# Two loads swapped, a stretch of the FFN in another array form, and the steps in a new order: retention followed by a gated FFN

## The chip, the cores and the metric

The kernel runs on one core of one Trainium2 chip. The metric is device microseconds of one execution, the median of three runs.

## The reference

Two operations follow each other. The first is a retention layer, written as a recurrence over 768 tokens for 4 sequences and 8 heads of 64 columns:

```python
for t in range(S):
    state = gamma * state + einsum('bhd,bhe->bhde', k[:, :, t], v[:, :, t])
    y[:, :, t] = scale * einsum('bhd,bhde->bhe', q[:, :, t], state)
```

The second is a feed-forward network on the 3072 resulting rows of 512 columns, with 1536 hidden columns: `out = (sigmoid(x @ w_gate) * (x @ w_val)) @ w_out`.

## The kernel before

**Tiling.** A tile `t` (0 to 5) is 128 tokens of each of the 4 sequences, so 512 rows of x. A pair `P` (0 to 11) is half a tile: the 128 tokens of two sequences; tile t has the pairs 2t and 2t+1, and a pair has two sequences c = 0, 1. Retention is computed chunk by chunk: scores of a chunk against itself, masked with the decay, times v (within the chunk), plus q times the state left by the chunks before.

**Queues.** Nothing is scheduled by a planner. The list `ORDER` holds one string for each tile, each word of it is a step, and the steps are issued in exactly that order; each engine (TensorE = PE, VectorE = DVE, ScalarE = ACT, GpSimd = POOL, the DMA queue of SyncE = SP) works off its own share of the list in order. A word is two letters and a number; `+` or `-` behind it moves it to the next or the previous tile (`dp02-` in the string of tile 1 works on tile 0). So the order of two steps on different engines matters only through what they wait for, the order of two steps on one engine always.

**The steps that the prediction speaks of:**

- `lk`, `lq`, `lv` P: load k, q, v of a pair with a DMA issued by POOL (L64). Eight such DMAs may be under way; the next issue waits for the eighth before it. Pairs 0 to 5 and all weights are loaded ahead of the list; the list itself loads pairs 6 to 11. `load_gate_val(s)` (L85) loads columns 256s to 256s+255 of w_gate and w_val, that is hidden blocks n = 2s and 2s+1; `load_out` (L89) loads w_out.
- k and q must be transposed. Pairs 0 to 3 are transposed on PE (`tp`, L178) and evicted by ACT (`te`); from pair 4 on, SP does it with DMA transposes (`xk`, `xq`, L197). `ho` P: POOL waits until the transposes of pair P have landed (L557), then issues the next loads.
- `sc` n: scores of pair n//2, sequence n%2, on PE (L216); `sd` P does both sequences. `mk`: mask on DVE (L221). `in`: q times the state, `ia`: masked scores times v, both on PE (L233, L239). `yo`: DVE writes the result into xT, the FFN's input (L254). `kt`: scaled k; `sm`, `zs`, `zo`: the state product on PE (L262), its sum on DVE, its copies on ACT.
- `gm` n, `vm` n: gate and value product of hidden block n for all 512 rows, 4 matmuls of 512 columns. `ag`/`av` n (first 256 rows) and `bg`/`bv` n (last 256 rows), used in tile 1: two hidden blocks, 8 matmuls of 256 columns. `sg`, `as`, `bs`: sigmoid on ACT; `mu`, `am`, `bm`: gate times value on DVE. From tile 3 on the value product of two blocks is made from seven half products `vp` g,1 to `vp` g,7 (a fast matrix product of Strassen's kind), put together by `vc` (ACT), `va` (DVE), `vf` (POOL, one of them DVE).
- `dp` i,1 to i,7: seven half products of the output product, for two of a tile's four row blocks, put together by `dc` (ACT), `da` (DVE), and stored by `ds` (SP). They need sums of hidden columns, `hs`/`hh` (DVE), and of w_out, `wp` (POOL) with `wc` (ACT). `dm`, `do`, `dt`: the plain output product, its copy and its store, for the other two row blocks of tile 0. `aw`: sums of w_val on POOL. `tt`: decay tables on POOL.

**Array form.** The 128 x 128 array can take a matmul as a whole (the profile writes `128*128`), as two column halves (`128*64`, two matmuls of 64 output rows side by side) or as two row halves (`64*128`). Scores use row halves; `in`, `ia`, `sm` use column halves. A plain FFN matmul can be made either way in `mm`:

```python
if not halves or plain:
    nc.tensor.matmul(o, left, right, ...)      # L285, 128*128
    return
for i in range(2):                              # L289, 128*64
    half = slice(i * D, (i + 1) * D)
    nc.tensor.matmul(o[half], left[:, half], right, ...)
```

`halves` is set by the first state product (`sm0`), `plain` by the last within-chunk product (`il11`): between the two every FFN matmul is made of column halves.

Of the kernel before, what the change touches and what calls it, by code (L numbers as in the profile page):

```python
# [17 lines left out]
def kernel(  # L18
# [147 lines left out]
    def new_qkT(P):  # L166
        qkT[P] = ld.tile([128, 2, 2, NP, C], BF16, tag="qkT", name="qkT", bufs=4)

    halves, plain, turned = [], [], {}

    def transpose(P, i, cs):
        tp = bank([128, 2 * NP, C], BF16).rearrange("d (c p) s -> d c p s", c=2)
        x = (kn, qn)[i][P].rearrange("s g d -> s (g d)")
        for c in cs:
            for p in range(NP):
                for lo, n in ((0, D), (D, D)) if halves else ((0, C),):
                    at_p = (c * NP + p) * C + lo
                    nc.tensor.transpose(tp[lo:lo + n, c, p, :], x[:, at_p:at_p + n], ident)  # L178
        turned[P, i] = tp
# [74 lines left out]
            nc.vector.tensor_tensor(o, y[P, c], taby[t], op=ALU.mult)  # L254

    def state(P):
        halves.append(P)
        zz[P] = pz.tile([128, 2, NP, D], F32, tag="z", name="z")
        for c in range(2):
            for p in range(NP):  # L260
                for i in range(2):
                    nc.tensor.matmul(zz[P][i * D:(i + 1) * D, c, p, :], heads(kt[P], c)[:, 2 * p + i, :],  # L262
                                     heads(vn[P], c)[:, 2 * p + i, :], start=True, stop=True, skip_group_check=True)
# [17 lines left out]
    gated = {}  # L281

    def mm(during, o, left, right, **kw):
        if not halves or plain:
            nc.tensor.matmul(o, left, right, skip_group_check=True, **kw)  # L285
            return
        for i in range(2):
# [315 lines left out]
        up(0, 0, which, 256, 512)  # L603
    up_sigmoid(0, 0, 256, 512)
    up_finish(0, 0, 256, 512)
    for s in range(3, NFF // 2):
        load_gate_val(s)
    load(2, "k", "q", "v")
    load(3, "k", "q", "v")
    for i in range(3):  # L610
        tile_tables(1, i)
    for s in range(4):
# [52 lines left out]
        "in": lambda t, n: inter(n // 2, n % 2),  # L665
        "sd": lambda t, P: [scores(P, c) for c in range(2)],
        "id": lambda t, P: [inter(P, c) for c in range(2)],
        "il": lambda t, P: plain.append([intra(P, c) for c in range(2)]),
        "ia": lambda t, n: intra(n // 2, n % 2),
        "sm": lambda t, P: state(P),  # L670
        "mk": lambda t, n: mask(n // 4, n // 2 % 2, n % 2),
# [1 line left out]
        "zs": lambda t, P: state_sum(P),  # L673
        "zo": lambda t, n: state_out(n // 2, n % 2),
    }
    ORDER = [
        "gm1 vm1 sg1 mu1 gm2 vm2 sg2 mu2 kt0 gm3 vm3 sg3 mu3 kt8 gm4 vm4 sg4 mu4 sm0 zs0 zo0 zo1 gm5 vm5 sg5 mu5  "
        "gm6 vm6 sg6 mu6 sm1 zs1 zo2 zo3 hh0 hh1 hh2 hh3 gm7 vm7 sg7 mu7 gm8 vm8 sg8 mu8 xk4 xq4 xk5 xq5 kt16  "
        "gm9 vm9 sg9 mu9 tp4 te4 tp5 te5 gm10 vm10 sg10 mu10 sc4 sc5 sm2 mk8 mk9 mk10 mk11 gm11 vm11 sg11 in4+  "
        "in5+ ia4+ ia5+ yo4+ yo5+ mu11 zs2+ kt24+ tp6+ te6+ tp7+ te7+",  # L680
        "ag0 av0 as0 am0 ag2 av2 as2 am2 sc6 sc7 sm3 mk12 mk13 mk14 mk15 zs3 ag4 av4 as4 am4 ag6 av6 as6 am6 in6  "
        "in7 ia6 ia7 yo6 yo7 zo4 zo5 ag8 av8 as8 am8 hh4- hh5- hh6- hh7- wp0 wp1 wp2 wp3 wc0 wc1 bg0 bv0 bs0 bm0  "
        "zo6 zo7 tt6 tt7 tt8 bg2 bv2 bs2 bm2 wp4 wp5 wp6 wp7 wc2 wc3 kt32 kt33 kt34 kt35 bg4 bv4 bs4 bm4 ag10  "
        "tt9 bg8 bs8 aw6+ dm2- bg6 bv6 bs6 as10 aw8+ bv8 kt37 hh8- hh10- bg10 sc8 wp8 kt45 bs10 sc9 bm8 kt39  "
        "kt38 bm6 dm3- wp9 aw4+ kt36 av10 in8 aw0+ kt43 wp10 ho5 sm4 sc11 mk16 mk19 do1- lk6 sc10 mk17 dp01-  "
        "aw9+ mk18 mk23 kt40 mk21 am10 dp02- tt10 hh9- dp05- mk22 zs4 hh11- dc05- lq6 in10 wc5 lv6 dp02 aw5+  "
        "mk20 lk7 ia8 lq7 in11 kt46 ia11 kt42 dp03- kt47 da05- dp06- ia10 dm6- dc06- in9 bv10 kt44 wc4 yo8 yo10  "
        "da06- dt1- hs0 yo11 ds06- kt41 sm5 lv7 ia9 dp07- tt11 bm10 dm7- yo9 zs5 hs8 zo9 xk6 hs4",
        "gm0 xq6- gm1 hs9- wp11- aw7 vm0 da07-- hs1- vm1 hs6- xk7- do3-- sg1 dt3-- hs2- sg0 zo10- aw1 aw3 hs3-  "
        "xq7- hs5- mu0 dp04-- dc04-- dp01- hs10- hs11- aw2 zo11- mu1 hi0- zo8- hs7- ds04-- aw10 aw11 aw12 aw13  "  # L690
        "aw14 aw15 aw16 aw17 aw18 aw19 dp05- dc05- da05- kt48 kt49 kt50 kt51 gm2 vm2 sg2 mu2 dp03- dp06- dc06-  "
        "da06- ds06- kt52 kt53 kt54 kt55 gm3 vm3 sg3 mu3 dp07- da07- ho7 lk8 lq8 lv8 tt12 tt13 tt14 lk9 lq9 lv9  "
        "gm4 vm4 sg4 mu4 dp04- dc04- ds04- sc12 sc13 sm6 mk24 mk25 mk26 mk27 zs6 gm5 vm5 sg5 mu5 kt56 kt57 kt58  "
        "kt59 dp11- dp12- gm6 vm6 sg6 mu6 dp15- dc15- da15- kt60 kt61 kt62 kt63 gm7 vm7 sg7 mu7 xk8 xq8 dp13-  "
        "dp16- dc16- da16- ds16- hs0 hs1 hs2 hs3 gm8 vm8 sg8 mu8 xk9 xq9 dp17- da17- hs4 hs5 hs6 hs7 gm9 vm9 sg9  "
        "mu9 dp14- dc14- ds14- sc14 sc15 in12 in13 ia12 ia13 sm7 mk28 mk29 mk30 mk31 yo12 yo13 zs7 zo12 zo13  "
        "gm10 vm10 sg10 mu10 kt64 kt65 kt66 kt67 in14 in15 ia14 ia15 yo14 yo15 zo14 zo15 gm11 vm11 sg11 mu11  "
        "kt68 kt69 kt70 kt71 hs8 hs9 hs10 hs11 xs0+ xs1+ xs2+ xs3+ dp01 dp11",
        "gm0 sg0 dp02- dp12- kt72 kt73 kt74 kt75 dp05- dc05- da05- dp15- dc15- da15- vp1 vp2 vp5 vc5 va5 ho9  "
        "lk10 lq10 lv10 lk11 lq11 lv11 tt15 tt16 tt17 dp03- dp06- dc06- da06- ds06- vp3 vp6 vc6 va6 vf6 dp13-  "  # L700
        "dp16- dc16- da16- ds16- dp07- da07- gm1 sg1 dp17- da17- dp04- dc04- ds04- sc16 sc17 sm8 mk32 mk33 mk34  "
        "mk35 zs8 dp14- dc14- ds14- vp7 va7 vf7 gm2 sg2 vp11 vp12 vp15 vc15 va15 gm3 sg3 vp13 vp16 vc16 va16  "
        "vf16 gm4 sg4 vp4 vf4 vp17 va17 vf17 kt76 kt77 kt78 kt79 sc18 sc19 in16 in17 ia16 ia17 sm9 mk36 mk37  "
        "mk38 mk39 yo16 yo17 zs9 zo16 zo17 gm5 sg5 vp21 vp22 vp25 vc25 va25 xk10 xq10 gm6 sg6 vp23 vp26 vc26  "
        "va26 vf26 gm7 sg7 vp14 vf14 vp27 va27 vf27 vp31 vp32 vp35 vc35 va35 xk11 xq11 hs0 hs1 gm8 sg8 vp24 vf24  "
        "vp33 vp36 vc36 va36 vf36 hs2 hs3 gm9 sg9 vp41 vp42 vp45 vc45 va45 vp37 va37 vf37 gm10 vm10 sg10 mu10  "
        "vp43 vp46 vc46 va46 vf46 vp34 vf34 hs4 gm11 vm11 sg11 vp47 va47 vf47 hs5 in18 in19 ia18 ia19 yo18 yo19  "
        "zo18 zo19 mu11 vp44 vf44 hs6 hs7 hs8 hs9 hs10 hs11 dp01 xs0+ dp11",
        "vp2 gm0 dp02- dp15- dp05- dp12- dc05- vp1 dp03- da05- dp06- dc15- da15- xs2 xs3 vp5 dw24 dp13- dc06-  "
        "da06- xs1 vc5 sg0 va5 dp16- dc16- gm1 da16- dp07- sd10 da07- mk43 dp17- dp04- sg1 vp11 vp3 dc04- da17-  "  # L710
        "vp15 vp12 mk41 vc15 mk40 dp14- dc14- vp13 vp6 va15 vp16 mk42 vc16 gm2 va16 gm3 sd11 vc6 sg2 va6 mk45  "
        "vp7 vp17 sg3 mk46 mk47 gm4 gm7 sg4 va17 vp21 va7 sg7 vp14 vp22 dw25 vp25 vf16 vf6 vp4 dw27 vf17 vc25  "
        "mk44 gm11 sg11 vf14 vf4 id10 va25 vp32 dw26 vp23 vf7 vp31 vp35 ia21 vc35 gm6 va35 vp26 yo21 gm5 ds04-  "
        "vp33 hs0 vc26 va26 vp36 ia20 vc36 va36 vf26 gm8 sg6 vp27 vp37 gm10 va27 yo20 vp41 sg8 vp45 va37 vp42  "
        "vp51 vp34 sg5 vp24 vf34 sg10 vp52 vf36 vp55 vc45 va45 vf24 vc55 vp43 vp46 gm9 hs1 vf27 hs3 vc46 va55  "
        "va46 vp53 vp56 vc56 id11 va56 vp47 vf37 sg9 vf46 va47 vf56 il11 vp57",
        "vp12 va57- yo23- vp44- vp54- vf57- vf54- vp1 vp2 dp01- yo22- dp11- gm2 sg2 vf44- hs4- vf47- gm0 xs0 vp5  "
        "hs8- xs2 dp15- gm1 hs5- vc5 dp05- hs7- sg0 dp12- hs9- vp11 hs2- hs11- va5 vp3 dc15- dp13- dc05- vp15  "
        "da15- dp16- xs1 vc15 vp6 vp13 sg1 vc6 dp02- va15 gm5 gm4 sg5 sg4 vp16 vc16 hs6- xs3 hs10- va6 dc16-  "
        "da05- gm3 dp03- sg3 va16 vp7 va7 vp21 da16- vf6 vf16 dp06- vp22 dc06- vp4 da06- vp17 gm6 va17 vp25  "  # L720
        "ds06-- vf4 vp32 vc25 dp17- dp07- vf7 vp31 vp35 sg6 da07- vp14 vp23 vp26 vf17 da17- vc35 dp14- vp33 va35  "
        "va25 vc26 vp36 vp42 va26 vc36 dp04- dc14- ds16- vp27 hs0 gm7 vp51 vf14 dc04- vp41 vp45 vc45 va27 vf26  "
        "va36 vp37 va37 gm8 vp43 vp34 vp46 sg7 hs2 ds16-- vp55 va45 vf27 vf34 sg8 vp52 gm10 hs1 vf36 vc55 vc46  "
        "vp53 hs3 vp56 va46 va55 gm9 vp47 vf37 vf46 vc56 va56 vp57 sg10 sg9 vf56 gm11 va47 va57 ds14- vp44 vp24  "
        "vp54 vf44 vf24 sg11 vf54 vf47 hs4 dp11 vf57 hs8 dp01 dp02 dp05 dp15 ds14-- dc05 hs5 hs9 hs11 hs7 dc15  "
        "hs6 dp12 dp13 da15 ds04- ds06- dp03 dp06 dp16 hs10 da05 dc03 da06 dc13 da16 dp07 da07 dp17 dp04 ds16  "
        "ds06 da17 dp14 ds07 dc04 dc14 ds17 ds14 ds04",
    ]
    for t, order in enumerate(ORDER):
        for s in order.split():  # L730
            at_t = t + s.count("+") - s.count("-")
            s = s.strip("+-")
            STEPS[s[:2]](at_t, int(s[2:]))


# [28 lines left out]
```

## Time and profile before

| | us |
|---|---|
| median of 3 runs | 223.9 |
| the runs | 220.94, 223.9, 224.31 |
| the profiled execution | 223.24 |
| its span, first to last instruction | 221.5 |
| PE busy in the span | 209.2 |
| POOL, DVE, ACT busy | 130.5, 158.7, 117.1 |

The granted TensorE clock is 1.00 in every stretch of 10 us from 20 to 210 us. PE starts the FFN at 15.3 us, the last matmul ends at 217.7 us. "Busy" counts an engine's instruction from start to end; since matmuls overlap, the pace of PE is read from one start to the next.

The loads around the change, as the trace has them (issue on POOL, landing):

| load | issued | landed |
|---|---|---|
| w_gate, w_val, slice 4 | 16.95, 18.48 | 26.94, 28.26 |
| w_gate, w_val, slice 5 | 19.22, 20.49 | 29.57, 31.98 |
| k, q, v of pair 2 | 21.87, 23.18, 24.50 | 33.78, 35.59, 37.42 |
| k, q, v of pair 3 | 25.84, 27.22, 28.83 | 39.16, 40.92, 41.88 |
| k, q of pair 6 | 67.41, 69.85 | 74.54, 76.31 |
| q of pair 7 | 74.00 | 82.41 |

### The profile page before, as it was taken

Reading aid. Unit: us, or ns where it says so; the run is one execution under the profiler, and the core shown is the slowest. Engines: PE = TensorE matmul, PEld = TensorE weight load, DVE = VectorE, ACT = ScalarE, POOL = GpSimd, SP = SyncE. Lnnn points to the kernel's source line nnn. Section 1 sums busy time; section 2 is a strip of 40 time slices with the busy share of each in tenths; the row PEclk is TensorE's granted clock in tenths of the full one; section 3 lists DMA queues with packets and bytes.
Section 4 is the critical chain, followed back from the end, with each engine's and each line's share of the span. In section 5 each row is a group of like instructions: output and inputs, shape, how many; then the busy total and the mean of one; then the engine's idle time right before and its main releaser. Section 6 shows DMA issues by size and latency. Waiting matters only on the chain.

```text
span 221.5 us, 7090 instructions
## 1 busy us (share of the span) xinstructions
PE 209.2 (94%) x3020; PEld 163.8 (74%) x3024; DVE 158.7 (72%) x330; ACT 117.1 (53%) x254; POOL 130.5 (59%) x149
## 2 busy tenths in 40 slices
PE   6678999999999999999979999999999999999993
PEld 6564455799989857666769977789867777687782
DVE  6764875988668996566976589898675695557761
ACT  7484375528853647454576367633454715546331
POOL 8976894789988975992006962570053660427700
PEclk9889999999999999999999999999999999999999
DMA  9999999999997999699993999700010000025005
GB/s 126 139 171 196 196 172 156 192 188 157 145 127 90 138 177 189 126 164 143 127 188 27 165 225 169 93 0 3 23 74 4 3 0 3 0 95 190 2 1 191
DMA packets 103999, 25.35 MB, mean 114 GB/s; under 512 B 93984, under 2 KB 101152, under 8 KB 103968
## 3 DMA queue, kind: packets, MB, share of 16 engines
q0 software_dynamic: 81248, 13.90, 83.3%
q1 hardware_dynamic: 22576, 10.88, 27.0%
q8 instruction: 23, 0.38, 0.7%
q10 hardware_dynamic: 144, 0.13, 0.2%
q14 instruction: 8, 0.07, 0.1%
HBM read 28.31 MB, written 6.29 MB: 156 GB/s over the span
## 4 chain that ended last, share of the span: by engine, by line
PE 79%; DMA 13%; DVE 3%; POOL 3%; issue 1%; ACT 0%; POOLq 0%; DVEq 0%
PE ff L289 54%; PE ff L285 17%; DMA qn<-in_q_dram 6%; DMA wg<-in_moe_w_gate_dram 4%; DMA vn<-in_v_dram 3%; PE ff L216 2%; PE ff L233 2%; PE ff L239 2%; PE z L262 1%; POOL kn L64 1%; DVE st L221 1%; DVE hs L461 1%; DVE xT L254 1%; POOL qn L64 0%; POOL kn L72 0%
## 5 line engine op out<-in xcount | busy, mean ns | idle before, releaser
L289 PE MATMUL ff<-xT,wg 128*64 128x512 bf16 (+1 forms) x536 | 56.5, 341 | 0.3 <-DVE xT L254 0.3
L309 ACT ACTIVATE gs<-ff 128x512 f32<-128x512 f32 (+1 forms) x61 | 35.5, 590 | 33.1 <-PE ff L289 21.8
L406 POOL TENSOR_TENSOR hT<-gs,scr 128x512 bf16<-128x512 f32 x17 | 21.7, 1289 | 41.4 <-DVE scr L400 27.9
L289 PE MATMUL ff<-xT,wv 128*64 128x256 bf16 (+1 forms) x448 | 41.6, 312 | 0.0
L289 PEld LDWEIGHTS <-wg 128*64 128x64 bf16 x536 | 30.4, 110 | 10.0 <-issue 0.4
L289 PEld LDWEIGHTS <-wv 128*64 128x64 bf16 x484 | 27.6, 110 | 9.9
L400 DVE TENSOR_TENSOR scr<-scr,ff 128x256 f32<-128x256 f32 x51 | 20.4, 417 | 12.2 <-ACT scr L393 4.9
L312 DVE TENSOR_TENSOR hT<-gs,ff 128x512 bf16<-128x512 f32 (+1 forms) x27 | 17.9, 664 | 14.8 <-PE ff L289 6.2
L221 DVE TENSOR_TENSOR st<-ff,maskd 128x512 bf16<-128x512 f32 x40 | 25.2, 684 | 2.7 <-PE ff L216 2.6
L289 PEld LDWEIGHTS <-hT 128*64 128x64 bf16 x384 | 21.2, 110 | 3.8
L515 DVE TENSOR_TENSOR ob<-p,ff 128x256 f32<-128x256 f32 x33 | 13.6, 418 | 13.0 <-ACT p L507 4.4
L285 PE MATMUL ff<-xT,wg 128*128 128x512 bf16 (+1 forms) x68 | 16.9, 366 | 1.7 <-ACT xT L252 0.9
L289 PE MATMUL ff<-wo,hT 128*64 128x256 bf16 (+1 forms) x216 | 16.7, 297 | 0.0
L209 ACT ACTIVATE kt<-kn,tabk 128x128 bf16<-128x128 bf16 x48 | 15.6, 391 | 0.1
L64 POOL DMA_DIRECT2D vn<-in_v_dram x12 | 14.0, 1165 | 2.0 <-DMA wo<-in_moe_w_out_dram 0.8
L275 ACT CAST zbd<-za 64x512 bf16<-64x512 f32 x20 | 12.3, 615 | 5.4 <-DVE za L269 3.1
L409 POOL TENSOR_TENSOR hT<-gs,scr 128x256 bf16<-128x256 f32 x17 | 12.4, 738 | 4.1 <-DVE scr L400 2.5
L64 POOL DMA_DIRECT2D kn<-in_k_dram x11 | 12.9, 1176 | 3.1 <-PE ff L289 1.8
L289 PEld LDWEIGHTS <-hs 128*64 128x64 bf16 x252 | 13.9, 110 | 1.1 <-DVE hs L461 0.5
L393 ACT COPY scr<-ff 128x512 f32<-128x512 f32 x17 | 10.0, 586 | 8.9 <-PE ff L285 5.7
L254 DVE TENSOR_TENSOR xT<-ff,taby 128x512 bf16<-128x512 f32 x20 | 13.1, 683 | 0.8 <-PE ff L239 0.8
L64 POOL DMA_DIRECT2D qn<-in_q_dram x11 | 12.7, 1158 | 1.3 <-DMA wo<-in_moe_w_out_dram 0.6
(108 smaller groups left out, 395.3 us busy)
## 6 DMA issues: line engine op xcount, KB each, us to landing
out_dram<-ob SPq DMA_DIRECT2D x22, 256.0 KB, 3.8
vn<-in_v_dram POOLq DMA_DIRECT2D x12, 256.0 KB, 12.3
kn<-in_k_dram POOLq DMA_DIRECT2D x11, 256.0 KB, 7.5
qn<-in_q_dram POOLq DMA_DIRECT2D x11, 256.0 KB, 9.6
wo<-in_moe_w_out_dram POOLq DMA_DIRECT2D x4, 384.0 KB, 13.1
wg<-in_moe_w_gate_dram POOLq DMA_DIRECT2D x5, 256.0 KB, 9.5
wv<-in_moe_w_val_dram POOLq DMA_DIRECT2D x5, 256.0 KB, 9.3
out_dram<-ob SPq DMA_DIRECT2D x3, 128.0 KB, 2.2
```

The source lines that it names most:

```text
L64: nc.gpsimd.dma_start(out=held[P], in_=src(x, P))
L209: nc.scalar.activation(to[:, :, h, :], x[:, :, h, :], AX.Copy, scale=tabk[:, P // 2, h:h + 1])
L221: nc.vector.tensor_tensor(st[P, c, i], sc[P, c][i], (mask0 if P < 2 else maskd[P // 2])[:, i], op=ALU.mult)
L254: nc.vector.tensor_tensor(o, y[P, c], taby[t], op=ALU.mult)
L285: nc.tensor.matmul(o, left, right, skip_group_check=True, **kw)
L289: nc.tensor.matmul(o[half], left[:, half], right, skip_group_check=True, **kw)
L309: nc.scalar.activation(gated[t, n1][:, lo:hi], us[t, n1, 0][:, lo:hi], AX.Sigmoid)
L312: nc.vector.tensor_tensor(hidden(t)[:, n1, lo:hi], gated[t, n1][:, lo:hi], us[t, n1, 1][:, lo:hi], op=ALU.mult)
L400: nc.vector.tensor_tensor(o, o, (b if n == 5 else ac)[:, :256], op=ALU.add)
L406: nc.gpsimd.tensor_tensor(h[:, 2 * g], s, vals[t, g][:, 0:2].rearrange("p two n -> p (two n)"), op=ALU.mult)
L409: nc.gpsimd.tensor_tensor(h[:, 2 * g + 1, 256:], s[:, 256:], vals[t, g][:, 2], op=ALU.mult)
L515: nc.vector.tensor_tensor(o, x, z, op=ALU.add)
```

## The change

Three things change; what is computed stays the same, and the list holds the same 1037 steps.

```diff
-    halves, plain, turned = [], [], {}
+    whole, turned = [True], {}
...
-                for lo, n in ((0, D), (D, D)) if halves else ((0, C),):
+                for lo, n in ((0, C),) if whole[0] else ((0, D), (D, D)):
...
     def state(P):
-        halves.append(P)
...
     def mm(during, o, left, right, **kw):
-        if not halves or plain:
+        if whole[0]:
...
-    for s in range(3, NFF // 2):
+    for s in range(3, NFF // 2 - 1):
         load_gate_val(s)
-    load(2, "k", "q", "v")
+    load(2, "k", "q")
+    load_gate_val(NFF // 2 - 1)
+    load(2, "v")
     load(3, "k", "q", "v")
...
-        "il": lambda t, P: plain.append([intra(P, c) for c in range(2)]),
+        "il": lambda t, P: [intra(P, c) for c in range(2)],
...
+    STEPS.update({n.upper(): f for n, f in STEPS.items()})
...
             s = s.strip("+-")
+            whole[0] = s[0].isupper()
             STEPS[s[:2]](at_t, int(s[2:]))
```

1. `load(2, "k", "q")` is issued ahead of slice 5 of w_gate and w_val; v of pair 2 behind it.
2. The form of an FFN matmul is now a matter of each step: capitals take the array as a whole. Capitals stand for the first products of tile 0 (as before), in tile 1 for one `ag` step and for the stretch from `AV8` to `BV6`, and from the last string on for nearly all FFN steps, with one `VP1` ahead of them.
3. From `sm0` on, every string has a new order. In tile 0 and tile 1 (the strings are cut):

```diff
-  "... sm0 zs0 zo0 zo1 gm5 vm5 sg5 mu5 gm6 vm6 sg6 mu6 sm1 zs1 zo2 zo3 hh0 hh1 hh2 hh3 gm7 vm7 sg7 mu7
-   gm8 vm8 sg8 mu8 xk4 xq4 xk5 xq5 kt16 gm9 vm9 sg9 mu9 tp4 te4 tp5 te5 gm10 vm10 sg10 mu10 sc4 sc5 sm2
-   mk8 mk9 mk10 mk11 gm11 vm11 sg11 in4+ in5+ ia4+ ia5+ yo4+ yo5+ mu11 zs2+ kt24+ tp6+ te6+ tp7+ te7+"
+  "... sm0 zs0 zo0 zo1 gm5 vm5 sg5 mu5 gm6 vm6 sg6 gm9 gm7 gm8 sg9 sm1 mu6 zs1 xk4 tp4 vm9 vm8 tp5 sg8
+   vm7 sg7 te4 gm10 te5 aw0++ hh0 tt7+ sc5 kt16 sc4 vm11 mu9 xq4 sm2 mu8 mu7 mk10 gm11 mk9 in5+ sg10 tp6+
+   in4+ mk11 ia5+ mk8 ia4+ wp0+ sg11 yo5+ te6+ yo4+ kt24+ vm10 mu10 zs2+ wp1+ hh1 tp7+ mu11 zo3 te7+"
...
+  "ag2 AG8 sc7 sc6 av2 ag0 as2 av4 zo2- ... in7 in6 ia6 as8 mk14 sm3 av0 as4 wp2 am2 yo6 ia7 AV8 tt9 yo7
+   as0 as6 zs3 BG4 am4 BG8 aw8+ BV4 aw6+ hh8- BG0 zo7 zo6 bs8 am0 BG2 zo5 aw9+ kt39 bs0 kt34 wc0 am8 wc1
+   BV0 BG6 wp4 wp3 wp5 BV8 AG10 xk5- am6 BG10 wp8 bm0 DM2- bs2 wp6 wp7 bs6 bs4 kt44 bm8 bm4 BV2 kt37 hh3-
+   BV6 hh4- bm2 bm6 dm3- bs10 kt36 sc9 as10 hh5- sc8 xq5- wc3 dp02- mk17 aw4+ kt38 tt8 mk16 wp9 bv10 kt35
+   mk19 mk18 dp01- do1- wp10 sc11 aw2+ kt47 hh9- zo4 dp05- wc2 mk23 kt41 wc4 kt32 hh7- ho5 kt42 av10 in8
+   hh11- dc05- dp03- ia8 sc10 mk22 ... lk6 wc5 in11 lq6 ... aw16+ am10 lv6 ..."
```

In the strings of tiles 2 and 3 the scores of one pair come apart (`sc17 ... vp6 gm1 sm8 dp07- sc16`, `sc18 ... gm5 ... sc19`), as `sc11` and `sc10` do in tile 1. On SP the store `ds06--` of tile 0 (list 2) moves from ahead of `xk6` to behind `xq6`, and `dt3--` from ahead of `xq7` to behind it. Counted over the built program, PE changes its array form 42 times instead of 31, and issues 2906 matmuls instead of 3024: 118 pairs of column halves become 118 whole matmuls.

## The prediction

> **What bounds the kernel now.** First the page's busy times and its chain of waits: is one engine the end, or do several alternate?
>
> ```profile
> PE 209.2 (94%) x3020; PEld 163.8 (74%) x3024; DVE 158.7 (72%) x330; ACT 117.1 (53%) x254; POOL 130.5 (59%) x149
> ```
>
> ```profile
> PE 79%; DMA 13%; DVE 3%; POOL 3%; issue 1%; ACT 0%; POOLq 0%; DVEq 0%
> ```
>
> PE is busy for 94% of the span, and the DMA share of the chain lies ahead of 35.6 us. So the change can win only what PE loses after 25.45 us, where the new order begins. The waits of PE by what ended them, those after 25.45 us:
>
> ```profile
> PE ff L239 <- issue: 1.4, 1, 1.4
> PE ff L178 <- DMA qn<-in_q_dram: 0.4, 1, 0.4
> PE ff L289 <- DVE xT L254: 0.3, 1, 0.3
> PE ff L289 <- DVE hs L461: 0.2, 1, 0.2
> ```
>
> That is all: four waits. What each costs is read from start to start in the timeline of PE (columns: start, length, engine, line):
>
> ```profile
> 34.62 0.61 PE L178 MATMUL ff<-ident,kn 128*64 128x128 bf16 x16
> 35.63 0.64 PE L178 MATMUL ff<-ident,qn 128*64 128x128 bf16 x16 [0.41 <-DMA qn<-in_q_dram]
> ...
> 40.49 0.61 PE L233 MATMUL ff<-qkT,zbd 128*64 128x128 bf16 x16
> 40.93 0.70 PE L239 MATMUL ff<-st,vn 128*64 128x128 bf16 x16
> 41.44 0.64 PE L178 MATMUL ff<-ident,kn 128*64 128x128 bf16 x16
> 41.89 0.63 PE L178 MATMUL ff<-ident,qn 128*64 128x128 bf16 x16
> 42.78 1.06 PE L289 MATMUL ff<-xT,wg 128*64 128x256 bf16 x16 [0.25 <-DVE xT L254]
> ...
> 45.39 1.07 PE L289 MATMUL ff<-xT,wv 128*64 128x256 bf16 x16
> 46.39 0.62 PE L216 MATMUL ff<-qkT 64*128 64x128 bf16 x16
> 46.94 0.44 PE L262 MATMUL z<-vn,kt 128*64 128x64 bf16 x16
> ```
>
> Sixteen column-half matmuls of 128 columns take 0.45 us start to start (41.44 to 41.89). So the wait for q of pair 2 cost 35.63 - 34.62 - 0.45 = 0.56, and that for xT 42.78 - 41.89 - 0.45 = 0.44. At 72.68 eight matmuls of 256 columns last 0.44 and the next starts at 73.47: 0.35 for the hidden sums. The large one:
>
> ```profile
> 110.77 0.39 PE L239 MATMUL ff<-st,vn 128*64 128x128 bf16 x7
> 112.54 0.47 PE L239 MATMUL ff<-st,vn 128*64 128x128 bf16 x9 [1.39 <-issue]
> ```
>
> Seven matmuls of one group, then nothing, then nine more: 112.54 - 110.77 - 0.20 = 1.57. Nothing in the profile released it, and the loader of weights stood still with it (1.55). The four sum to 2.92.
>
> **The change, part by part.**
>
> *Loads.* Landings follow each other at 1.8 us for a k or q of 256 KB (31.98, 33.78, 35.59); behind slice 4 (28.26) k and q of pair 2 land at 30.1 and 31.9, then slice 5 at 33.2 and 35.6 (its own steps 1.3 and 2.4), v at 37.4 as before. PE's work up to there, summed from 25.45 with 0.865 for a `gm` or `vm` (25.73, 26.59), 0.45 for a `tp`, 0.25 for `sm`: `tp4` at 32.1, `tp5` at 34.3, `gm10` at 35.6, `vm11` at 37.3, `sm2` at 38.2. Each stands 0.8 to 2.4 behind its load. The 0.56 goes; if slice 5 came 1.7 later than that, `vm11` would wait.
>
> *Tile 0 to 1.* What is late next is xT. DVE hands on a 512-column operation every 0.60 (four masks last 2.48 at 65.77) and `kt16` every 1.15. From `zs1` (32.1) its list runs through `kt16`, `mu9`, `mu8`, `mu7`, the masks from 37.0 on, ends them at 39.4, and `yo4` at 41.6; PE needs it for `ag2` at 41.9. The 0.44 goes, with 0.3 to spare; uncovered it costs what the spare lacks.
>
> *Hidden sums.* In the new list `dp03-` starts at 71.3 by PE's sum, and `hh9`, `hh7`, `hh11` (0.2 each) stand behind the four masks that follow `sc8` (66.9): 4 x 0.60, one mask for `sc11`, three sums: 70.6. The 0.35 goes, spare 0.7. The stretch is full: DVE has about 13 of 16 us there, so `in11` behind `am10` and `dm6-` behind `yo8` come within 0.2 of waiting. New waits of this kind: between 0 and 1.5 (five places at 0.3); I take 0.3, near the lower end, since in the old order, with DVE at 12.83 of 14 us from 66 to 80, only one such place cost anything.
>
> *The wait without a releaser.* What it is, the trace doesn't say. Of the page's queues, the one for instructions moved 23 packets for 6044 instructions of PE and its loader, one in 263; the wait falls in a stretch with four DMA transposes under way (99.77 to 117.75). If PE was waiting for its own program there, a list with 236 instructions fewer, cut at other places, may meet it or not, and there are four such stretches. Bounds: gone (-1.57) or twice (+1.57). I take it as gone, since in three of the four stretches it didn't show, and keep it as a rival.
>
> *The array as a whole.* 118 pairs become single matmuls. Pace of a pair of 256 columns: 0.109 (16 in 0.87 at 43.65); of a whole one, six in 0.66 at 184.95: 0.109. For 512 columns four last 0.865 in either form (24.49, 26.59). So nothing is won in the stream itself. What costs is the change of form. Into row halves: the products at 45.39 last 0.87, the scores start at 46.39, so 0.13 is lost. Out of them: 16 score matmuls last 0.55 to the next start, against 0.44 for 16 of the same columns in column halves (40.49): 0.11. Whole to column halves: 24.49 + 0.865 to 25.45, 0.095. Back: 178.08 + 0.45 to 178.62, 0.09. The new list changes form 42 times, not 31: three score pairs come apart (`sc11`/`sc10`, `sc17`/`sc16`, `sc18`/`sc19`: three ways in, three out), and `AG8`, the long stretch and the early `VP1` add five. Sum: 3 x 0.13 + 3 x 0.11 + 5 x 0.095 = 1.2. Between whole and row halves there is no clean row; 0.13 is taken, bounds 0 and 0.5. The Trainium skill (TensorEngine Tiling (Array Packing), Key Properties) states that a change of tiling mode drains the array, which speaks against this part, and the rows agree; by TensorE: Matmul & The Clock Gate (Step-by-step) a drain is about 128 cycles, 53 ns at 2.4 GHz, and eleven would be 0.6.
>
> *POOL, SP and the later loads.* `wp10` needs a buffer that ACT empties in `wc2`, and in the new list `wc2` stands behind `do1-`, `kt47` and `zo4`. `do1-` waits for `dm3-`, which ends at 66.0; then 0.59 + 0.33 + 0.62 + 0.62: 68.2. Queued behind `wp10` on POOL are `aw2`, `ho5` and the loads of pairs 6 and 7. With `wp10` at 1.2, `aw2` at 0.67 and `ho5`, `lk6` issues at 70.4 instead of 67.41, and `lq7`, with three `aw` and a `tt` between, at 77.7 instead of 74.0. In the trace 20 us pass from `lk6` to the landing of `xq6` (87.29): now 90. `sc13`, by PE's sum, wants it at 94: spare 4. `ho7` then lets `lk8` go at about 95 (before 92.17), `xq8` lands 21 later, at 116; `sc17` is at 121: spare 5. Nothing waits. `ds06--` behind `xq6` and `dt3--` behind `xq7` on SP leave at some 85 and 90; DVE's `da07-` and `da15-`, which need their buffers, come at 92 and 96, after landings of 3 to 5 us. Cost nil while these spares hold, and DVE with all its masks waits where they don't.
>
> Sum: 223.24 - 0.56 - 0.44 - 0.35 - 1.57 + 1.2 + 0.3 = 221.8. The profiled run stands 0.7 below the median of its three (223.9), so for a median I write 222.2.
>
> **The rivals.**
>
> *The wait without a releaser comes again* (or another in its place): 222.2 + 1.57 = 223.8. For it: the same transposes, the same queues. Against: it showed once in four stretches.
>
> *The loads of pairs 6 to 9 come too late.* POOL's list is longer ahead of `ho5`; they decide once `lk6` is 3 + 4 = 7 us later than before, and each us past that is a us of PE at `sc13`, with `zs`, `yo` and the gates behind it. 11 us later gives 222.2 + 4 = 226; over 2% slower it is from 13 us on. For it: POOL is at 12.68 of 14 us from 66 to 80 and gains a wait there. Against: the spare.
>
> *Many small waits and dearer changes of form*: the upper bounds, 1.5 and 1.7 (1.2 + 0.5) in place of 0.3 and 1.2, with the large wait gone: 223.9; with it back, 225.5.
>
> *Over 2% faster.* Even with no new wait and drains of 0.6 the sum is 220.9. It needs a median at the low end of the spread, as the 220.94 of before stands 3 below its median: 219.2. For it only this spread.
>
> **How the numbers follow.** 2% is about what a measurement of this kernel can tell from no change (its three runs spread over 1.5%); it is 4.5 us: faster lies below 219.4, slower above 228.4. Chances: forecast 0.46 at 222.2; the large wait again 0.24 at 223.8; late loads 0.10 at 226, 0.04 of it over 228.4; small waits 0.10 at 223.9 to 225.5, 0.04 of it over 228.4 for what I don't see; over 2% faster 0.10 at 219.2. Faster 0.10; slower 0.08; same 0.82. The range runs from 219.6, just above the spread's low end, to 226.2, which takes in the late loads at 11 us; it leaves out 0.2.
>
> **What would show it.** `tp5` and the first `ag` of tile 1 without a wait, the latter 0.8 earlier, at 42.0; PE with no wait at the hidden sums; the `128*128` rows of tile 1 at 0.109 for 256 columns; about 0.1 lost at each change of form; `lk6` near 70.4 and `xq6` ahead of `sc13`. It would be wrong if PE shows a wait of over a us for a DMA or DVE between 60 and 125 us, or if the whole matmuls run at another pace.

## The result, and the profile after

The changed kernel takes 223.92 us by the median of 21 runs (222.83 to 225.66), the kernel before, beside it, 223.01 (220.94 to 225.60). The ratio is 1.0055, 95% interval 1.0033 to 1.0076: some 1.2 us longer, inside the 2% and inside the range, but on the other side of the forecast, which had the change 1.7 below the 223.9 known then. The ratio, and every ratio and median span below, goes by the fast runs alone, without those over 1.5% above the fastest run of their kernel. The profiled execution took 223.84, its span 221.4 (before 223.24 and 221.5).

The page of the changed kernel, busy times and the chain by engine:

```profile
PE 210.8 (95%) x2906; PEld 160.7 (73%) x2906; DVE 154.9 (70%) x330; ACT 116.5 (53%) x254; POOL 131.7 (59%) x149
...
PE 86%; DMA 4%; DVE 4%; POOL 3%; ACT 1%; issue 0%; POOLq 0%
```

PE is still the bound, a little more so. DMA's share of the chain fell from 13% to 4%, DVE's rose. The waits of PE by what ended them (total, times, longest), without those of the first 20 us:

```profile
PE ff L284 <- DVE hT L328: 0.9, 1, 0.9
...
PE ff L239 <- DMA vn<-in_v_dram: 0.2, 1, 0.2
```

The second lies at 16 us. So all four waits that the prediction struck out are gone, and one stands in their place. In PE's timeline (start, length, engine, line):

```profile
34.29 0.61 PE L178 MATMUL ff<-ident,qn 128*64 128x128 bf16 x16
34.74 1.03 PE L288 MATMUL ff<-xT,wv 128*64 128x512 bf16 x8
...
41.55 0.61 PE L178 MATMUL ff<-ident,qn 128*64 128x128 bf16 x16
42.09 1.06 PE L288 MATMUL ff<-xT,wg 128*64 128x256 bf16 x16
...
54.63 1.04 PE L284 MATMUL ff<-xT,wv 128*128 128x256 bf16 x8
55.50 1.04 PE L284 MATMUL ff<-xT,wg 128*128 128x256 bf16 x8
57.45 1.03 PE L284 MATMUL ff<-xT,wg 128*128 128x256 bf16 x8 [0.92 <-DVE hT L328]
```

`tp5` at 34.29 and the first `ag` at 42.09 start without a wait. Eight whole matmuls of 256 columns take 0.87 (54.63 to 55.50), as they did in column halves. Then 57.45 - 55.50 - 0.87 = 1.08 is lost, waiting for a gate. DVE's timeline shows what stood ahead of that gate, and GpSimd's what ran meanwhile:

```profile
53.31 0.68 DVE L328 TENSOR_TENSOR hT<-gs,ff 128x512 bf16<-128x512 f32 x1
53.91 2.90 DVE L460 TENSOR_TENSOR hs<-hT 128x256 bf16<-128x256 bf16 x1
56.73 1.87 DVE L328 TENSOR_TENSOR hT<-gs,ff 128x512 bf16<-128x512 f32 x3
```

```profile
53.76 0.66 POOL L339 TENSOR_TENSOR ws<-ws,wv 128x256 bf16<-128x256 bf16 x1
54.39 1.14 POOL L443 TENSOR_TENSOR wt<-wo 128x512 bf16<-128x512 bf16 x1
55.50 1.15 POOL L443 TENSOR_TENSOR wt<-wo,scr 128x512 bf16<-128x512 bf16 x1
58.04 1.16 POOL L443 TENSOR_TENSOR scr<-wo 128x512 f32<-128x512 bf16 x1 [1.39 <-ACT wt L446]
```

The step `hh8-`, a sum of 256 elements that takes 0.28 at other places, took 2.90. It began 0.15 into `aw9`, and ended 0.16 after GpSimd's run of `aw9`, `wp4`, `wp3` was over. The gates `am0`, `am8` and `am6` stand behind it on DVE, and PE's next gate product waits until the first of them has read its PSUM bank (`ff`).

### The profile page after: what moved, and what is told of

Same layout as the page of the kernel before. It is cut to its first block, busy times and chain, and to the rows that moved or that the text cites. A ratio compares the mean times of both kernels' runs of the same rounds, so it can differ in the third digit from the quotient of the medians.

```text
span 221.4 us, 6848 instructions
## 1 busy us (share of the span) xinstructions
PE 210.8 (95%) x2906; PEld 160.7 (73%) x2906; DVE 154.9 (70%) x330; ACT 116.5 (53%) x254; POOL 131.7 (59%) x149
## 4 chain that ended last, share of the span: by engine, by line
PE 86%; DMA 4%; DVE 4%; POOL 3%; ACT 1%; issue 0%; POOLq 0%
PE ff L288 52%; PE ff L284 25%; DMA vn<-in_v_dram 4%; PE ff L216 3%; PE ff L239 2%; PE ff L233 2%; DVE hs L460 2%; PE z L261 1%; PE ff L178 1%; DVE hT L328 1%; ACT kt L209 1%; POOL kn L64 1%; POOL vn L64 1%; POOL qn L64 1%; POOL kn L72 0%; POOL qn L72 0%
## 5 line engine op out<-in xcount | busy, mean ns | idle before, releaser
L288 PE MATMUL ff<-xT,wg 128*64 128x512 bf16 (+1 forms) x408 | 47.1, 363 | 0.0
L288 PE MATMUL ff<-xT,wv 128*64 128x256 bf16 (+1 forms) x352 | 35.7, 324 | 0.0
L288 PEld LDWEIGHTS <-wg 128*64 128x64 bf16 x408 | 22.8, 110 | 11.7
L284 PE MATMUL ff<-xT,wg 128*128 128x256 bf16 (+1 forms) x136 | 25.7, 323 | 2.4 <-ACT xT L252 0.9
L288 PEld LDWEIGHTS <-wv 128*64 128x64 bf16 x388 | 21.2, 110 | 8.0 <-issue 0.2
L288 PEld LDWEIGHTS <-hT 128*64 128x64 bf16 x372 | 20.2, 110 | 3.7 <-issue 0.2
L284 PEld LDWEIGHTS <-wg 128*128 128x128 bf16 x136 | 13.0, 98 | 8.8 <-issue 2.2
L209 ACT ACTIVATE kt<-kn,tabk 128x128 bf16<-128x128 bf16 x48 | 16.7, 395 | 4.0 <-PE z L261 3.4
L284 PE MATMUL ff<-xT,wv 128*128 128x256 bf16 (+1 forms) x96 | 15.8, 290 | 0.0
L288 PE MATMUL ff<-wo,hT 128*64 128x256 bf16 (+1 forms) x204 | 15.5, 292 | 0.0
```

The costliest lines, as they stand in the source:

```text
L209: nc.scalar.activation(to[:, :, h, :], x[:, :, h, :], AX.Copy, scale=tabk[:, P // 2, h:h + 1])
L288: nc.tensor.matmul(o[half], left[:, half], right, skip_group_check=True, **kw)
```

## The experiments

Besides the ratio, two numbers are used for each: the span by the median of the runs (kernel before 220.8, changed kernel 221.7), and by how much the time exceeds the span (before: 1.66 to 1.78 in every run; changed: 1.66 to 2.80, mean 2.03).

**The same kernel again** (`b_again`, no edit).

> The kernel before once more, nothing changed, for a second profile and a second set of times. Theory A (the wait of 1.57 without a releaser at 111 belongs to one execution and not to the kernel): it is not in this profile, or stands at another place; the rest of PE's waits (0.41 at tp5, 0.25 at the first ag, 0.2 at the hidden sums) stand as they were; ratio to the kernel before 1.000. Theory B (it belongs to the kernel): it stands at 110 to 113 again, 1.2 to 1.6 us.

Ratio 0.9984 (0.9951 to 1.0016). PE's timeline, the two places where it waited without a releaser:

```profile
62.17 1.58 PE L289 MATMUL ff<-xT,wv 128*64 128x256 bf16 x25
64.83 0.62 PE L289 MATMUL ff<-xT,wv 128*64 128x256 bf16 x7 [1.08 <-issue]
...
111.82 0.39 PE L239 MATMUL ff<-st,vn 128*64 128x128 bf16 x7
112.66 0.47 PE L239 MATMUL ff<-st,vn 128*64 128x128 bf16 x9 [0.45 <-issue]
```

Theory B holds, with a twist: the wait is back behind the same seventh matmul of `ia15`, shorter (112.66 - 111.82 - 0.20 = 0.64), and there is a second, of 1.3, which the first profile did not show. The place belongs to the kernel, the length to the execution. The smaller waits do not all stand as they were: the one for the hidden sums is there (0.3), but `tp5` starts without one (34.87 to 35.31, 0.44). At the first `ag` the list has none either, yet from `ia4` to that `ag` (40.59 to 42.43, three groups of 0.45) PE loses 0.49 in small pieces, as much as in before (40.93 to 42.78).

**One part alone: the loads** (`b_loads`).

```diff
-    for s in range(3, NFF // 2):
+    for s in range(3, NFF // 2 - 1):
         load_gate_val(s)
-    load(2, "k", "q", "v")
+    load(2, "k", "q")
+    load_gate_val(NFF // 2 - 1)
+    load(2, "v")
```

> The kernel before with one part of the change: k and q of pair 2 ahead of weight slice 5. Theory A (the prediction's): the wait of PE at tp5 goes, and the time falls by 0.2 to 0.6 us (ratio 0.9975 to 0.999), less than 0.56 if the wait for xT at the first ag grows by what came earlier. Rival: xT takes it all, ratio 1.000, with the wait at 42.78 grown from 0.25 to 0.7.

Ratio 0.9999 (0.9968 to 1.0030). PE's wait at `tp5` is gone from the profile, as it was in `b_again` without any edit, and the first `ag` comes at 42.07. The runs show no gain, though the interval does not exclude 0.56 (a ratio of 0.9975). The wait behind the seventh matmul of `ia15` is there again (0.75).

**One part alone: the whole array** (`b_whole`), the old order with `ag8 ... bg10` of tile 1 in capitals.

```diff
-  ag8 av8 as8 am8 ... bg6 bv6 bs6 as10 aw8+ bv8 kt37 hh8- hh10- bg10
+  AG8 AV8 as8 am8 ... BG6 BV6 bs6 as10 aw8+ BV8 kt37 hh8- hh10- BG10
```

> The kernel before with one part of the change: all products of tile 1 from its first ag8 to bg10 on the array as a whole, in the old order. Theory A (the prediction's): the pace is the same and one more change of form comes in, +0.1 us, ratio 1.000 to 1.001. Rival (the whole form itself costs, by its weight loads of 128 columns or by slower banks): +0.5 us or more, ratio above 1.002, with rows of 128*128 at over 0.112 per 256 columns start to start.

Ratio 0.9941 (0.9920 to 0.9963), span 219.25. Neither had it: 1.3 us shorter. The pace is as expected; the profile has no wait without a releaser anywhere, and the spans lie between 218.8 and 220.0, where those of before, run beside it, lie between 219.2 and 222.5. The sizes agree: the profiles of before and `b_again` less their waits without a releaser would have spans of 219.9 and 219.7, and the profile of `b_whole` has 219.8. So the term of 1.57 of the prediction comes here with the form, the order being the old one.

**Where the wait without a releaser stands** (`b_shift`): `keep_on(30)` becomes `keep_on(42)` in the kernel before.

> The kernel before with 12 more matmuls of the identity at the start, where PE waits for q anyway: every later instruction of PE stands 24 further on in its program. Theory F: the wait without a releaser, which stood behind the seventh matmul of ia15 in two profiles of before and in that with the loads alone, is tied to a place in the program's stream and stands 24 instructions earlier, behind some eleven matmuls of in15, 0.4 us or more. Rival (it is tied to ia15's operands or to what the other engines do then): it stands behind the seventh matmul of ia15 again, or nowhere while the time is shorter by 1 us.

One run, 223.29. In PE's timeline:

```profile
62.78 0.93 PE L288 MATMUL ff<-xT,wv 128*64 128x256 bf16 x13
64.28 1.28 PE L288 MATMUL ff<-xT,wv 128*64 128x256 bf16 x19 [0.57 <-issue]
```

It shows at the other of the two places, and there the test is clean: in `b_again` PE stopped behind the 25th matmul of this step, here behind the 13th, 24 instructions earlier. In the stream of PE's instructions the two stand at the same number, 1730. Those at `ia15` stand at 3266. A later run (`best`) stopped at 3010. All three leave a remainder of 194 when divided by 256, and the trace has PE's program come in packets of 16 KB, 22 to 24 for some 6,000 instructions. At 109.13 such a packet starts in the profile of before, 1.8 ahead of the stop. In `b_shift` the expected place at `ia15` shows no stop.

The traces of all 14 profiles bear this out. With the n-th packet set against instruction 194 + 256 n, PE's loader of weights reaches 301 such places. The six stops of these profiles are the six places that it reached soonest behind the end of that packet, 0.6 to 0.8 us; at one more, reached 1.4 behind (number 962 in `best`), it stood for 0.3; at the 294 others, reached 1.5 or more behind, no gap is over 0.12. So PE stops where its program comes late. Why the packet's record ends 0.6 to 0.8 ahead of the stop is not shown.

**Parts together** (`b_whole_loads`): the diffs of `b_loads` and `b_whole` in the old order.

> The change without its new order: the old order with both other parts, the loads of pair 2 ahead of slice 5 and the whole array in tile 1's stretch. If the parts add: the whole form alone gave 0.9941 and the loads alone 0.9999, so 0.994; the new order then costs the other 1.0055 - 0.994, or 2.5 us. Rival (the new order is what makes the loads pay, so that its cost is smaller than it looks): as before, 0.994, but PE's wait at the first ag of tile 1 grown by what tp5's wait was. If the loads pay once PE's program is no longer late: 0.992 to 0.993.

Ratio 0.9933 (0.9907 to 0.9960), span 219.0. The parts add, within what the intervals tell, and the profile shows no longer wait at the first `ag` (42.04). PE's list has no wait at all after 20 us; only the small pieces ahead of that `ag` are there (0.50 from 40.19). So in the old order with the other two parts, little is left that the new order could take away. What is left of the change, its new order, costs (1.0055 - 0.9933) x 222.5 = 2.7 us.

**The sum moved** (`a_hh8`), in the changed kernel.

```diff
-  ... BG8 aw8+ BV4 aw6+ hh8- BG0 ... as10 hh5- sc8 ...
+  ... BG8 aw8+ BV4 aw6+ BG0 ... as10 hh5- hh8- sc8 ...
```

> The changed kernel with the hidden sum hh8 moved from the place ahead of am0, where GpSimd runs sums back to back, to the place behind hh5, where GpSimd is idle. Theory A (VectorE's sum of two SBUF tensors is held for as long as GpSimd's sums run on): it takes 0.28 in place of 2.90, am0, am8 and am6 come 2.6 earlier, PE's wait of 0.9 at 57.45 goes, and the time falls by about 1 us (ratio to the kernel before 1.000 to 1.002 where the changed kernel had 1.0055). Rival (the 2.9 us have another cause, such as the operands' banks, or PE's wait of 0.9 is covered later): the sum is as long at its new place, or the time stays at 1.004 to 1.006.

Ratio 0.9973 (0.9947 to 0.9999), span 220.2. The sum at its new place, in DVE's timeline:

```profile
65.24 0.28 DVE L460 TENSOR_TENSOR hs<-hs,hT 128x256 bf16<-128x256 bf16 x1
65.44 0.28 DVE L460 TENSOR_TENSOR hs<-hT 128x256 bf16<-128x256 bf16 x1
```

The list of PE's waits has none after 20 us. The span falls by 1.5, more than the 1.08 of the one profile, which was among the shorter of its runs.

**GpSimd moved instead** (`a_pool`): `aw8+`, `aw6+` and `aw9+` go behind `wp9`; `hh8-` stays.

```diff
-  ... BG8 aw8+ BV4 aw6+ hh8- BG0 zo7 zo6 bs8 am0 BG2 zo5 aw9+ kt39 ... mk16 wp9 bv10
+  ... BG8 BV4 hh8- BG0 zo7 zo6 bs8 am0 BG2 zo5 kt39 ... mk16 wp9 aw8+ aw6+ aw9+ bv10
```

> The changed kernel with hh8 where it was and three of GpSimd's sums (aw8, aw6, aw9, 1.95 us) moved out of the run of sums ahead of 56.7 into its idle time behind wp9. Theory P (hh8 is held until GpSimd pauses): GpSimd's run ends near 54.7, hh8 ends there, after 0.8 to 1.2 us and not 2.9; PE's wait of 0.9 at 57 is gone or under 0.3; span 220.2 to 220.6 by the median (the changed kernel 221.7, with hh8 moved 220.2). Rival (hh8 is long by its operands or its place in VectorE's list): still over 2 us, span 221.5 or more.

Ratio 0.9994 (0.9965 to 1.0024), span 220.0. DVE's row, and GpSimd's last ahead of its pause:

```profile
54.47 0.80 DVE L460 TENSOR_TENSOR hs<-hT 128x256 bf16<-128x256 bf16 x1
```

```profile
52.85 1.14 POOL L443 TENSOR_TENSOR wt<-wo 128x512 bf16<-128x512 bf16 x1
53.97 1.15 POOL L443 TENSOR_TENSOR wt<-wo,scr 128x512 bf16<-128x512 bf16 x1
```

The same sum at the same place of DVE's list now ends 0.15 behind the end of GpSimd's run (55.12), after 0.80, and PE's wait is gone. For `hh8` theory P is shown from both sides. The span is that of `a_hh8`; the ratio is dearer in part by the excess over the span (mean 1.90 against 1.76), and the two intervals overlap.

That a sum is held until GpSimd pauses is not the rule, though. Two other sums in the changed kernel, DVE's rows and GpSimd's:

```profile
62.35 0.47 DVE L460 TENSOR_TENSOR hs<-hT,hs 128x256 bf16<-128x256 bf16 x1
62.74 0.75 DVE L460 TENSOR_TENSOR hs<-hT 128x256 bf16<-128x256 bf16 x1
```

```profile
61.51 1.16 POOL L443 TENSOR_TENSOR wt<-wo,scr 128x512 bf16<-128x512 bf16 x1
62.62 0.72 POOL L339 TENSOR_TENSOR ws<-wv 128x256 bf16<-128x256 bf16 x1
63.30 1.08 POOL L157 TENSOR_TENSOR taby<-taby,tabz 128x512 f32<-128x512 f32 x1
```

Each ended 0.15 behind the end of one GpSimd operation (62.67, 63.34), with the next one already running. Why `hh8` was held over three operations (over four in `a_cols`, 3.33 us) and these over one is not shown.

**The price of a change of form** (`b_whole_forms`): in the last tile of `b_whole` ten products in lower case, each between whole ones.

```diff
-  DP05- ... DP13- ... VP13 ... VP16 ... VP21 ... VP17 ... DP17- ... VP14 ... VP33 ... VP27
+  dp05- ... dp13- ... vp13 ... vp16 ... vp21 ... vp17 ... dp17- ... vp14 ... vp33 ... vp27
```

> The old order with the whole array in tile 1's stretch, and in the last tile ten single products out of a stretch of whole ones made in column halves: twenty changes of form more, 64 instructions more, nothing else. Theory H (a change costs PE 0.10 to 0.14 us, as the rows of the profiles show from start to start): 2.0 to 2.8 us longer than the kernel with the whole stretch alone, ratio 1.003 to 1.007 against before. Rival (a change costs a drain of about 53 ns): 1.1 us longer, 0.999. Rival (it overlaps the other waits there): 0.994 to 0.996.

Ratio 1.0065 (1.0034 to 1.0097), span 221.9 against 219.25. Theory H: 2.65 / 20 = 0.13 for one. In PE's timeline:

```profile
190.73 0.82 PE L284 MATMUL ff<-wo,hs 128*128 128x256 bf16 x6
191.38 0.38 PE L284 MATMUL ff<-xs,ws 128*128 128x256 bf16 x2
191.69 0.41 PE L288 MATMUL ff<-xT,wv 128*64 128x256 bf16 x4
192.04 0.83 PE L284 MATMUL ff<-wt,hs 128*128 128x256 bf16 x6
```

Two whole matmuls should take 0.22 and take 0.31 to the next start, four halves should take 0.22 and take 0.35: 0.09 on the way in, 0.13 on the way back. Ten times both are 2.2; the rest of the 2.65 is not placed.

**Without the whole array** (`a_cols`): the changed kernel with tile 1's list in lower case.

> The changed kernel with tile 1's long stretch back in column halves (236 instructions of PE and its loader more). Theory F (PE stops now and then because its program comes late, and the whole form, with half the instructions per us, is what ended that): waits of 0.5 to 1.6 us without a releaser come back at one place or more between 60 and 125 us, less 0.4 for four changes of form that are gone; time 0.3 to 1.5 us longer than the changed kernel (ratio 1.007 to 1.012 against the kernel before) and a wider spread. Rival G (it is the new order that ended them): no such wait, and 0.4 us shorter than the changed kernel (ratio 1.003 to 1.004).

Ratio 1.0083 (1.0053 to 1.0113), span 222.4. (It has three changes of form fewer, not four.) The time is what theory F gave, but its row is missing: this profile, the shortest of its seven runs, has no wait without a releaser, only that for `hT`, now 1.36. So this run does not tell F from G; `b_whole`, where the form changed and the order didn't, speaks for F.

**The end of PE's program** (`a_tail`): `keep_on(30)` becomes `keep_on(24)` in the changed kernel.

> The changed kernel with 6 warm-up matmuls fewer, so that PE's program ends 12 instructions earlier. In the changed kernel the time exceeds the span by 1.66 to 2.80 (mean 2.03), in before by 1.71 throughout. Theory T (the end of PE's program falls just behind a boundary of 256 instructions, where a block more has to come, as the fetch at 223.07 shows; 195 is the remainder of its 5827 instructions, stalls were seen at a remainder of some 190): with a remainder of 183 the excess is 1.7 in every run, the time 0.3 shorter on the mean, the span as before (221.7 by the median). Rival (the excess has to do with something else in the new order): it varies as before.

Ratio 1.0066 (1.0036 to 1.0096): it is no lower than the changed kernel's 1.0055 (the medians are 223.53 against 223.92, the intervals overlap), but the excess is 1.65 to 1.75 in all twelve runs, and the span 221.85. Theory T holds for the excess. The changed kernel's 5827 instructions end with number 5826, and 5826 again leaves 194: one instruction stands in a block of its own. In the profile a packet of 16 KB starts at 223.07, behind the span's end, and the excess is 2.44; only `b_shift` has such a packet too, with an excess of 2.69, and its last instruction, 6087, stands five behind a boundary. In the twelve profiles without one the excess is 1.65 to 1.85. What that packet brings is not shown. The kernels of 5827 and 5828 instructions all have an excess that varies (longest 1.95 to 2.80); those of 5815, 5816, 5892, 6063 and 6064 stay below 1.8. The mean cost is 0.3.

**Meant as the fastest** (`best`): `b_whole_loads` with `keep_on(24)`.

> The old order with the loads of pair 2 ahead of slice 5, the whole array in tile 1's stretch and 6 warm-up matmuls fewer: meant as the fastest of all. The same with all warm-up matmuls had 0.9933, spans of 219.0 by the median and an excess of the time over the span of 1.66 to 2.46 (mean 1.83). Theory T: excess 1.7 in every run, ratio 0.992 to 0.993. Rival (fewer warm-up matmuls leave PE's clock lower at the start): 0.3 or more longer, ratio over 0.994.

Ratio 0.9932 (0.9903 to 0.9961). The excess is steady at 1.7, as theory T has it, and the gain is lost again: the span is 219.6 and spreads from 218.3 to 220.7. PE's timeline says why:

```profile
109.74 0.28 PE L239 MATMUL ff<-st,vn 128*64 128x128 bf16 x3
111.60 0.58 PE L239 MATMUL ff<-st,vn 128*64 128x128 bf16 x13 [1.58 <-issue]
```

Twelve instructions fewer at the start moved the boundary at number 3010 into `ia15`, among the shortest matmuls of the kernel, and PE stopped for 1.77. So the whole form does not rule the stops out; by this account it had moved the boundaries to better places and halved the instructions per us in its stretch; which of the two did more was not tried. `best` and `b_whole_loads` are equal by what can be measured, and both beat the two kernels of the change.

**Fewer changes of form** (`a_fewer`): `a_hh8` with `AG8` of tile 1 and the lone first `VP1` of the last list in lower case (20 instructions more by the count of the built program, not 40).

> The changed kernel with hh8 moved and two single products back in column halves (AG8 of tile 1 and the VP1 that stands alone in the last list): three changes of form fewer, 40 instructions more. Theory H (0.13 us for each change): span 219.8 by the median against 220.2 with hh8 moved alone. Rival (what is left of the new order's cost is not in the changes of form): 220.2 or more. The excess of the time over the span may vary here (remainder 235), so the spans are compared.

Ratio 1.0043 (1.0019 to 1.0068), span 221.6: 1.4 longer, a miss. PE did what theory H said: its last matmul ended at 216.11, 0.56 ahead of `a_hh8`'s 216.67. The rest was lost behind it, on SP's queue:

```profile
213.87 0.81 SPq L520 DMA_DIRECT2D out_dram<-ob  x2
214.78 2.60 SPq L524 DMA_DIRECT2D out_dram<-ob  x2
217.50 0.37 SPq L526 DMA_DIRECT2D out_dram<-ob  x1
```

In `a_hh8` the two issues of L524 take 0.89 and the last store leaves at 216.44. Here they take 2.60, while a packet of PE's program is under way (214.73, 1.8 long). That the packet held them up is not shown.

## Why the prediction was wrong

By medians of the span: 220.8 before, -1.55 for the whole array, -0.25 for the loads, +1.2 for the new order without `hh8`, +1.5 for `hh8` held up, 221.7 after; and +0.3 behind the span.

*The step that failed* is the term of new waits in "Hidden sums": "between 0 and 1.5 (five places at 0.3); I take 0.3". One wait alone took 1.5 by the median (1.08 in the profile), at a place that was not among those looked at. What hid it is in the same paragraph: the sums are put at "0.2 each", as if their length were a constant of their shape. The profile of before had the sign. Two `hs` rows of 256 elements in DVE's timeline of before:

```profile
70.83 0.28 DVE L461 TENSOR_TENSOR hs<-hs,hT 128x256 bf16<-128x256 bf16 x1
...
72.23 1.19 DVE L461 TENSOR_TENSOR hs<-hT,hs 128x256 bf16<-128x256 bf16 x1
```

One operation in two lengths, 4 to 1, begs for a cause; the prediction credited the wait behind the second (0.35 at 73.47) and didn't ask. That one ended 0.53 behind a sum of GpSimd's, while GpSimd was issuing a load; its cause stays open. An earlier row of the same profile shows the cause, with GpSimd's rows beneath:

```profile
54.56 1.13 DVE L461 TENSOR_TENSOR hs<-hs,hT 128x256 bf16<-128x256 bf16 x1
```

```profile
54.27 1.27 POOL L444 TENSOR_TENSOR wt<-wo 128x512 bf16<-128x512 bf16 x1
55.50 1.20 POOL L444 TENSOR_TENSOR scr<-wo 128x512 f32<-128x512 bf16 x1
```

It ended 0.15 behind GpSimd's operation (55.54), as `hh8` and the sums at 62 us of the changed kernel did behind theirs.

*A second step failed with it*: gains were credited that were not there to win. The 0.56 at `tp5` is not in `b_again`, the same kernel without an edit. The 0.35 of the hidden sums is in `b_again`, but no longer in `b_whole_loads`, in the old order (twelve matmuls of 256 columns from 72.00 to 72.65). Only the 0.44 ahead of the first `ag` was left to the new order, and it had ten more changes of form to pay, 1.3 at the measured price: 0.9 together, where it cost 1.2 without `hh8`. That the changes make up most of this is a sum, not a test, and the remaining 0.3 is not placed.

*The large wait gone* was right, and so was its guess that PE's program comes late there, cut at other places. That no boundary of the new list fell where it hurts was luck, since nothing in the prediction counted them: `best` lost its gain by twelve instructions fewer. "It showed once in four stretches" was too kind: the next profile showed it twice. By `b_whole` the gain is 1.3, against 1.57 less one change of form, 1.44.

*The changes of form* were right in kind. At 2.65 / 20 each, eleven cost 1.46 and not 1.2, if the six into and out of row halves cost what the others do, which no run tried. The Trainium skill (TensorE: Matmul & The Clock Gate, Step-by-step) puts a drain at about 128 cycles, 53 ns at 2.4 GHz as an estimate, which would give 1.1 for the twenty of `b_whole_forms`; 2.65 was measured, and the measurement decides. The pace of 0.109 for 256 columns held.

*The loads*: the waits at `tp5` and at the first `ag` are gone as predicted, the `ag` at 42.09 for 42.0. The 0.56 does not show in the time: the loads alone gave nothing that the runs show, with the whole array 0.25 of span. `lk6` left at 71.32 (70.4 predicted) and nothing waited for the later loads.

*The rivals.* Late loads fell. The large wait did not come back in the profile. The measured time is that of "many small waits and dearer changes" (223.9) and near that of the large wait again (223.8); the number fits both by chance, for there was one long wait in place of many, and the large one was gone. The 0.3 at the end of PE's program stood in no case. The forecast's median has a slip as well: the sum is 221.8 for a profiled run said to stand 0.7 below its median, which makes 222.5; 222.2 was written.

## What to carry to other kernels

Before an operation is moved, look for rows of its shape with two lengths and find what makes the long one; here a cheap DVE sum of two SBUF tensors ahead of the work that frees PE's banks was dear where GpSimd ran sums back to back. Before a wait is credited, look for it in a second profile of the same kernel. A wait of PE without a releaser that recurs at the same instruction number, with lengths that vary, was here its program coming late: count instructions modulo 256, and keep the boundaries and the program's last instruction out of tight places. Test the parts of a change one by one: here two parts won 1.5 us and the third lost 2.7.

## What the runs showed of the hardware

DVE's sum of two SBUF tensors was held over three GpSimd operations in a row, 2.90 for 0.28, and over one in other places (1.13 at 54.56 before, 0.75 at 62.74 after), each time to 0.15 behind the end of a GpSimd operation. The Trainium skill (SBUF — State Buffer, Who interferes with whom) states that a DVE instruction with two SBUF inputs contends with a GpSimd instruction that reads SBUF, that the contention is an exclusive lock, and that the order of issue decides who blocks. The traces agree that DVE's sum blocks; that it can be held beyond the operation it met, to the third's end, the section does not say.

PE's program comes in packets of 16 KB. PE stopped for 0.6 to 1.8 six times in five profiles, and once more for 0.3, each time where the instruction's number leaves 194 when divided by 256 and the packet ahead had ended less than 1.5 before. The Trainium skill (Runtime: NRT & Kernel Launch, Instruction fetch mechanics) has blocks of 16 KiB, 256 instructions, and calls the cost of a boundary mostly hidden; the first agrees, the second did not hold here. Why a packet starts late in one execution and not in the next stays open.

A change between the whole array and column halves cost PE 0.13 on the mean of twenty.
